# Windowed attention before two gated layers: split float32r products and DMA transposes, against native float32 products and TensorE transposes

## The chip, the cores and the metric

One Trainium2 chip, one of its cores. The metric is the device time of one execution in microseconds (us); of several executions the median is taken. TensorE (PE in the profile; PEld is its weight load), VectorE (DVE), ScalarE (ACT), GpSimd (POOL) and the DMA queue of SyncE (SP) work side by side and wait for each other by semaphores.

## What is computed

Attention over 4 batches and 8 heads, 576 positions of 64 features, with a causal window of 128 and a linear bias by distance; then two gated layers on 2304 tokens of 512 features. All in float32.

```python
scores = scale * np.matmul(q, k.transpose(0, 1, 3, 2))
mask = (rel >= 0) & (rel < window)              # window = 128
scores = np.where(mask, scores + bias[None], -1000000000.0)
attn = np.exp(scores - np.max(scores, axis=-1, keepdims=True))
attn = attn / (np.sum(attn, axis=-1, keepdims=True) + 1e-09)
x = np.matmul(attn, v)                          # to 2304 x 512
x = (x @ w_a) * (x @ w_b) @ w_out               # d_ff 1536
out = ((x @ w1) * (x @ w2) @ w3) @ w_out2       # d_ff 1024
```

## The kernel before

The attention goes by units: a unit is one batch and two neighbouring heads (`units`, 16 of them), the two heads side by side on the 128 partitions. A unit has five query blocks (`NB`), of 128 queries, the last of 64; block 0 sees one block of keys, the others two (`window`). In the last block the two heads share one tile (`nj` is 1). The blocks of a unit are taken in three runs, `RUNS = ((0, 1), (2, 3), (4,))`, so there are 48 steps, and `attention_ops` (line 652) writes the program as a pipeline over steps. In step n stand:

- what was left from the step before: the evictions of the transposed q and k (`parted`), and `pv_out` of an older run;
- `scores` and `exps` of run n, then `norms` and `probs` of run n - 1;
- the transposes of a third of the next unit's q and k (`trans` in `prep`), and loads;
- at `None`, filler: matmuls of the first weight group of the first gated layer (`Filler`, `FILL` = 2.4 us a step by its own costs), as soon as that group's weights are converted and enough tokens of x are ready; lines 546 (`g1`) and 572 (`g2_two`);
- `pv` of run n - `LAG`.

Beside the steps `side.turn()` converts weights of 64 bits to float32 (`convert`, lines 107 to 126).

Every float32 operand of a TensorE product is split into a high part in float32r and the rest. For q and k: `parted` (lines 273, 274) copies the transposed block with ScalarE to `qkh` and subtracts with VectorE to `qkl`; `scores` (line 312) adds lo·hi, hi·lo and hi·hi. The two heads stand on partitions 0 to 63 and 64 to 127 of the array. `step_exps` (lines 338, 344) adds the bias and takes the extreme value with VectorE, then the exponential with ScalarE, which also sums. `norms` (357, 360) makes the reciprocals. `probs` multiplies by them and writes the result in two float16 halves into `pp` (372, 376, 378); one DMA transpose per block (line 383, SP's queue) turns `pp` into `pt`. `pv` (line 409) takes v as three bfloat16 parts (`v_parts`, made by GpSimd at line 72) as weights and `pt` as the moving operand: five terms per key block and head, the two heads in the two halves of the array's columns. `pv_out` (423, 424) evicts to `x_hi` and `x_lo`.

Accumulation tiles in PSUM: `ps_s` has three banks (scores), `ps_t` three (tile `tr`: transposed q and k, and the output of `pv`), `ps_g` two (filler and `keep_warm`, line 353, which runs idle products in the first three units).

Behind the attention the rest of the filler runs, then the other nine weight groups in the same manner with 512 tokens per tile, and a product of the last two weights, `w34`, which is made on the way.

Of the kernel before, what the change touches and what calls it, by code (L numbers as in the profile page):

```python
# [34 lines left out]
LAG = 3  # L35
# [7 lines left out]
def attention_moe_moe(ctx, tc, q, k, v, w_a, w_b, w_o, w_1, w_2, w_3, w_o2, out):  # L43
# [10 lines left out]
    PSC = 2.0 ** 15  # L54
# [133 lines left out]
    v_raws = [raw_p.tile([P, NB, P], F32, name=f"v_raw{i}") for i in range(3)]  # L188

    def consts():  # L190
        nc.gpsimd.memset(ident, 0.0)
        nc.gpsimd.affine_select(
            out=ident, in_=ident, pattern=[[-1, P]], base=0, channel_multiplier=1,
            compare_op=ALU.not_equal, fill=1.0,
        )

        rel = raw_2.tile([P, 2 * P], F32, name="rel")
        nc.gpsimd.iota(
            rel, pattern=[[1, 2 * P]], base=-P, channel_multiplier=-1,
            allow_small_or_imprecise_dtypes=True,  # L200
        )
# [13 lines left out]

        for j in range(2):
            nc.sync.dma_start(
                out=relb2[j * LAST:(j + 1) * LAST],
                in_=relb.rearrange("p (h j) c -> p h j c", j=2)[0:LAST, :, j, :],
            )  # L220
        for t in [t for ts in raws for t in ts] + v_raws:
            nc.vector.memset(t[:, NB - 1, :], 0.0)
# [7 lines left out]
    def load_unit(u, which=(0, 1, 2)):  # L230
        b, hp = units[u]
        for x in which:
            s = (q, k, v)[x][b, 2 * hp:2 * hp + 2]
            t = raw_of(u)[x] if x < 2 else v_raws[u % 3]
            for j in range(2):
                nc.sync.dma_start(
                    out=t[:, 0:NB - 1, j * D:(j + 1) * D],
                    in_=s[j, 0:(NB - 1) * P, :].rearrange("(c p) d -> p c d", p=P),
                )
            if x:  # L240
                nc.sync.dma_start(
                    out=t[0:LAST, NB - 1, :].rearrange("p (j d) -> p j d", j=2),
                    in_=s[:, (NB - 1) * P:S, :].rearrange("j p d -> p j d"),
                )
                continue

            for j in range(2):
                o = slice(j * D, (j + 1) * D)
                nc.sync.dma_start(out=t[o, NB - 1, o], in_=s[j, (NB - 1) * P:S, :])
# [4 lines left out]
    qk, vS = {}, {}  # L254

    def prep(u):


        def part(n):
            o = slice(parts[n][0][2], parts[n][-1][2] + P)  # L260
            hold = []

            def trans():
                if n == 0:
                    qk[u] = [tr_p.tile([P, 2 * NB * P], F32R, name=f"qk{x}") for x in "hl"]
                ps = ps_t.tile([P, W], F32, name="tr")[:, 0:o.stop - o.start]
# [11 lines left out]
        def v_parts():  # L278

            vr = v_raws[u % 3]  # L280
            r1 = tr_p.tile([P, NB, P], F32, name="v1")
            v2 = tr_p.tile([P, NB, P], BF16, name="v2")
            upper = [t.bitcast(BF16).rearrange("p c (f t) -> p c f t", t=2)[:, :, :, 1] for t in (vr, r1)]
            vS[u] = upper + [v2]
            sub(nc.gpsimd, r1, vr, upper[0])
            sub(nc.gpsimd, v2, r1, upper[1])

        return [part(n) for n in range(len(parts))] + [(v_parts, None)]
# [10 lines left out]
    def scores(run):  # L299
# [4 lines left out]
        for u, i in run:  # L304
            hi, lo = qk[u]
# [13 lines left out]
    def exps(run):  # L319
        st = sm_p.tile([P, 4, 2 * len(run)], F32, name="st", bufs=4)  # L320
        at = 0
        for u, i in run:
            nj = window(i)[3]
            live[u, i]["st"] = st[:, :, at:at + nj]
            step_exps(u, i)
            at += nj
        live[run] = st[:, :, 0:at]

    def step_exps(u, i):
# [5 lines left out]
        st = d["st"]  # L335
        for j in range(nj):
# [4 lines left out]
                accum_out=st[:, 0, j:j + 1],  # L341
# [13 lines left out]
    def norms(run):  # L355
        st = live.pop(run)
        nc.vector.tensor_scalar(
            out=st[:, 2], in0=st[:, 1], scalar1=1.0e-9, scalar2=1.0 / PSC, op0=ALU.add, op1=ALU.mult
        )
        nc.vector.reciprocal(out=st[:, 3], in_=st[:, 2])  # L360

    def probs(u, i):
        m, n, nb, nj = window(i)
        d = live[u, i]
        pe, st = d["pe"], d["st"][:, 3]
        pp = sm_p.tile([P, 2 * 2 * 2 * P], F16, name="pp", bufs=5)[:, 0:2 * nj * n].rearrange(
            "p (a b c) -> p a b c", a=nj, b=2
        )

        for j in range(nj):  # L370
            if i == 0:
                nc.vector.tensor_scalar(
                    out=pp[:, j, 0, :], in0=pe[:, j, :n], scalar1=st[:, j:j + 1], scalar2=None, op0=ALU.mult
                )
            else:
                nc.scalar.activation(pp[:, j, 0, :], pe[:, j, :n], ACTF.Copy, scale=st[:, j:j + 1])
        for j in range(nj):
            nc.vector.scalar_tensor_tensor(  # L378
                out=pp[:, j, 1, :], in0=pe[:, j, :n], scalar=st[:, j:j + 1], in1=pp[:, j, 0, :],
                op0=ALU.mult, op1=ALU.subtract,  # L380
            )
        t = sm_p.tile([P, 8 * P], F16, name="pt", bufs=6)[:, 0:2 * nj * n]
        nc.sync.dma_start_transpose(
            out=t.rearrange("p (g m) -> p g m", m=P), in_=pp.rearrange("p a b c -> p (a b c)")
        )

        order = "p (a b c m) -> p a b c m" if nj == 2 else "p (b c a m) -> p a b c m"
        d["pt"] = t, t.rearrange(order, a=2, b=2, c=nb)
# [4 lines left out]
    def pv(run):  # L393


        ps = outs[run] = ps_t.tile([P, W], F32, name="tr")
        at = 0
        for u, i in run:
            vs = vS[u]
            m, n, nb, nj = window(i)  # L400
            t, pt = live.pop((u, i))["pt"]
            terms = [
                (max(i - 1, 0) + g, g, hl, z)
                for g in range(nb) for hl, z in ((0, 2), (1, 1), (1, 0), (0, 1), (0, 0))
            ]
            for x, (kb, g, hl, z) in enumerate(terms):
                for j in range(2):
                    c = slice(j * D, (j + 1) * D)
                    nc.tensor.matmul(  # L409
                        ps[c, at:at + m], vs[z][:, kb, c], pt[:, j, hl, g, :],  # L410
                        start=(x == 0), stop=(x == len(terms) - 1),
                    )
            at += m
            if u < WARM_UNITS and m == P:
                keep_warm(WARM, t[:, 0:4 * P])

    def pv_out(run):
# [4 lines left out]
        ps = outs.pop(run)[:, :m]  # L422
        nc.scalar.activation(x_hi[:, hp, o], ps, ACTF.Copy, scale=1.0 / PSC)
        nc.vector.scalar_tensor_tensor(
            out=x_lo[:, hp, o], in0=ps, scalar=1.0 / PSC, in1=f32(x_hi[:, hp, o]),
            op0=ALU.mult, op1=ALU.subtract,
        )
# [224 lines left out]
    def attention_ops():  # L652

        late = []
        for n in range(NR + LAG):
# [5 lines left out]
            if 1 <= n <= NR:  # L661
                ops.append(lambda r=runs[n - 1]: norms(r))
# [22 lines left out]
            if k == RU - 1 and u + 1 < NU:  # L685
                ops.append(trans[RU][0])
# [39 lines left out]
    for f, g in prep(0):  # L726
        f()
        if g:
            g()
# [3 lines left out]
    warm = sm_p.tile([P, 8 * P], F16, name="pt", bufs=6)[:, 0:2 * P]  # L733
    nc.vector.memset(warm, 0.0)
    keep_warm(10, warm)
# [62 lines left out]
```

## Time and profile before

| | us |
|---|---|
| median of 3 runs (993.99 to 998.30) | 995.94 |
| the profiled execution | 995.97 |
| its span, first to last instruction | 994.2 |
| PE busy in the span | 953.7 (96%) |
| DVE busy | 533.0 (54%) |
| ACT busy | 430.4 (43%) |
| POOL busy | 399.5 (40%) |

The page gives for each engine the busy time in the span; then the span in 40 slices, where each digit is a busy share in tenths (for PEclk the TensorE clock that was granted, in tenths of full speed). The end of a matmul is modelled and matmuls overlap, so that PE's rate is read from the starts of neighbouring matmuls. "SPq" is the issue of a DMA on SP's queue. The chain of waits is followed back from the last instruction, at each step to what released it.

### The profile page before, as it was taken

To read this page: it belongs to the slowest core of one execution; us is meant where nothing else is said; L and a number is where in the kernel's file an instruction comes from. 1 tells how busy PE (TensorE), PEld (TensorE's weight loads), DVE (VectorE), ACT (ScalarE), POOL (GpSimd) and SP (SyncE) were. 2 spreads that over 40 slices of the span, in tenths; PEclk is the share of its full clock that TensorE was granted. 3 is DMA by queue.
4 is the path that set the end of the run, shared out by engine and by line. 5 is a ranking of instruction groups with operands and counts; after the bars stand their busy time and mean duration, and the time that the engine had idled before them with its cause. 6 is when DMAs were issued, how large, how long until landed. Compare 5 with 4: busy or idle time off the path is not lost.

```text
span 994.2 us, 16251 instructions
## 1 busy us (share of the span) xinstructions
PE 953.7 (96%) x6162; PEld 802.6 (81%) x6162; DVE 533.0 (54%) x1188; ACT 430.4 (43%) x1003; POOL 399.5 (40%) x329
## 2 busy tenths in 40 slices
PE   8889898888999999999999999999999999999998
PEld 6558787777988788888888888888888888888886
DVE  5979877775689734566474463442442442422222
ACT  5768867775554434434443342343421321311110
POOL 4344122221688423545362362584741631611111
PEclk9968999998999999999999999999999999999999
DMA  5797786764433222323341240120120120000012
GB/s 131 163 185 154 140 140 134 141 127 85 134 121 106 85 96 84 108 75 106 97 126 59 69 139 22 43 85 1 42 85 1 51 78 1 22 1 1 26 65 101
DMA packets 160079, 85.21 MB, mean 86 GB/s; under 512 B 128001, under 2 KB 148993, under 8 KB 160001
## 3 DMA queue, kind: packets, MB, share of 16 engines
q1 hardware_dynamic: 160000, 84.18, 34.1%
q8 instruction: 48, 0.79, 0.3%
q14 instruction: 31, 0.25, 0.1%
HBM read 58.20 MB, written 8.91 MB: 68 GB/s over the span
## 4 chain that ended last, share of the span: by engine, by line
PE 79%; DMA 7%; DVE 6%; ACT 3%; issue 3%; POOL 1%; SPq 1%; POOLq 0%; ACTq 0%; DVEq 0%
PE mm L546 44%; PE mm L583 11%; PE mm L598 10%; PE mm L462 4%; DMA pt<-pp 4%; PE s L312 3%; PE tr L409 3%; PE tr L269 2%; DVE pp L378 1%; PE mm L572 1%; DVE ca L121 1%; DMA raw<-in_moe_w_a 1%; DVE ca L117 1%; POOL ca L126 1%; PE mm L454 1%
## 5 line engine op out<-in xcount | busy, mean ns | idle before, releaser
L72 POOL TENSOR_TENSOR gl<-g,gh 128x512 fp32r<-128x512 f32 (+1 forms) x108 | 123.9, 1148 | 312.4 <-ACT gh L556 312.1
L553 DVE TENSOR_TENSOR g<-a,mm 128x512 f32<-128x512 f32 (+1 forms) x108 | 64.1, 594 | 212.8 <-PE mm L546 189.8
L126 POOL TENSOR_TENSOR ca<-ca,ce 128x512 int32<-128x512 int32 x76 | 101.3, 1333 | 141.2 <-ACT ce L110 68.6
L556 ACT ACTIVATE gh<-g 128x512 fp32r<-128x512 f32 (+1 forms) x108 | 60.2, 558 | 175.6 <-DVE g L553 175.6
L546 PE MATMUL mm<-x_hi,wlA 128*128 128x512 f32 (+1 forms) x464 | 107.5, 350 | 0.0
L551 ACT ACTIVATE a<-mm 128x512 f32<-128x512 f32 (+1 forms) x108 | 56.0, 519 | 117.5 <-PE mm L546 117.4
L546 PE MATMUL mm<-x_lo,whA 128*128 128x512 f32 (+1 forms) x464 | 104.0, 345 | 0.0
L546 PE MATMUL mm<-x_hi,whA 128*128 128x512 f32 (+1 forms) x464 | 102.9, 343 | 0.0
L546 PE MATMUL mm<-x_hi,wlB 128*128 128x512 f32 (+1 forms) x400 | 99.1, 370 | 2.1 <-DVE g L553 0.8
L546 PE MATMUL mm<-x_lo,whB 128*128 128x512 f32 (+1 forms) x400 | 98.5, 368 | 0.0
L546 PE MATMUL mm<-x_hi,whB 128*128 128x512 f32 (+1 forms) x400 | 98.1, 368 | 0.0
L114 DVE TENSOR_SCALAR ca<-ca 128x512 f32<-128x512 f32 x76 | 46.3, 610 | 91.8 <-ACT ca L107 90.6
L546 PEld LDWEIGHTS mm<-x_lo,whA 128*128 128x128 f32 x464 | 78.1, 192 | 10.5
L546 PEld LDWEIGHTS mm<-x_hi,wlA 128*128 128x128 f32 x464 | 77.7, 192 | 10.8 <-issue 0.4
L546 PEld LDWEIGHTS mm<-x_hi,whA 128*128 128x128 f32 x464 | 77.3, 191 | 10.2
L546 PEld LDWEIGHTS mm<-x_hi,wlB 128*128 128x128 f32 x400 | 70.8, 188 | 15.6 <-ACT a L551 1.3
L107 ACT ACTIVATE ca<-raw 128x512 f32<-128x512 f32 x76 | 50.7, 668 | 72.1 <-DMA raw<-in_moe_w 38.2
L587 DVE TENSOR_TENSOR acc<-acc,mm 128x512 f32<-128x512 f32 (+1 forms) x100 | 61.9, 629 | 36.9 <-PE mm L583 36.6
L546 PEld LDWEIGHTS mm<-x_lo,whB 128*128 128x128 f32 x400 | 71.1, 189 | 12.6
L546 PEld LDWEIGHTS mm<-x_hi,whB 128*128 128x128 f32 x400 | 71.0, 189 | 12.5
L121 DVE SCALAR_TENSOR_TENSOR ca<-raw,ca 128x512 int32<-128x512 int32 x76 | 79.9, 1052 | 1.8
L110 ACT ACTIVATE ce<-raw 128x512 int32<-128x512 uint32 x76 | 50.9, 670 | 60.0 <-POOL ca L126 24.9
(104 smaller groups left out, 1868.7 us busy)
## 6 DMA issues: line engine op xcount, KB each, us to landing
raw<-in_moe_w SPq DMA_DIRECT2D x32, 512.0 KB, 3.7
raw<-in_moe_w_out SPq DMA_DIRECT2D x20, 512.0 KB, 3.6
raw<-in_moe_w_a SPq DMA_DIRECT2D x12, 512.0 KB, 3.6
raw<-in_moe_w_b SPq DMA_DIRECT2D x12, 512.0 KB, 3.6
out<-acc SPq DMA_DIRECT2D x18, 256.0 KB, 2.0
q_raw<-in_q SPq DMA_DIRECT2D x32, 128.0 KB, 2.9
k_raw<-in_k SPq DMA_DIRECT2D x32, 128.0 KB, 2.7
v_raw<-in_v SPq DMA_DIRECT2D x32, 128.0 KB, 2.9
```

The source lines that it names most:

```text
L72: eng.tensor_tensor(out=out, in0=a, in1=b, op=ALU.subtract)
L107: nc.scalar.activation(a, f32(hw), ACTF.Abs)
L110: nc.scalar.activation(e, lw, ACTF.Copy, scale=2.0 ** -29)
L121: nc.vector.scalar_tensor_tensor(out=ai, in0=hw, scalar=-(1 << 30), in1=ai, op0=ALU.bitwise_and, op1=ALU.bitwise_or)
L126: nc.gpsimd.tensor_tensor(out=ai, in0=ai, in1=es[0], op=ALU.add)
L546: nc.tensor.matmul(p, w[:, z, kk, :], x[:, kk, o], start=(y == 0), stop=(y == len(terms) - 1))
L551: nc.scalar.activation(a, ps[0], ACTF.Copy)
L553: nc.vector.tensor_tensor(out=gg, in0=a, in1=ps[1], op=ALU.mult)
L556: nc.scalar.activation(gh, gg, ACTF.Copy)
L583: nc.tensor.matmul(p, w, x, start=(y == 0), stop=(y == len(terms) - 1))
L587: nc.vector.tensor_tensor(out=ya, in0=ya, in1=p, op=ALU.add)
L598: nc.tensor.matmul(p, x, w, start=(y == 0), stop=(y == len(terms) - 1))
```

## The change

q and k are evicted once, in float32 (`qk`), by ScalarE or VectorE, and not split. A score is one native float32 product in place of three float32r products. The exponentials are not normalised and not split: `probs` transposes them in float32 with TensorE into a tile `tr`, from which ScalarE (blocks 1 to 3) or VectorE (blocks 0 and 4) evicts them to `pt`. `norms` is gone, and so is the sum in the exponential. v stays as loaded, in rows of 66 per head, of which the last two hold 1.0; `pv` takes `pt` as weights and v as moving operand, so that queries come out on partitions, with the sum of their exponentials in column 64. VectorE adds 1e-9, takes the reciprocal and multiplies into `y`. `pv_out` turns `y` back with TensorE, two transposes for a run of two blocks, or for the last block one native product with two stacked identities (`pair`), into the tile in which `pv`'s output stood, and evicts as before. `LAG` goes from 3 to 2. GpSimd sets the columns of ones, `y_last` and `pair` at the start.

On PE, in the middle of the attention, where a run's scores end and a `pv` begins (`s` is the score tile, `v_844`, `v_845` the lower parts of v), before:

```order
L312 MATMUL s<-qkl,qkh 128x256
L312 MATMUL s<-qkh 128x256
L312 MATMUL s<-qkh,qkl 128x256
L312 MATMUL s<-qkl,qkh 128x256
L312 MATMUL s<-qkh 128x256
L409 LDWEIGHTS v_845
L409 MATMUL tr<-pt,v_845 64x128
L409 LDWEIGHTS v_845
L409 MATMUL tr<-pt,v_845 64x128
L409 LDWEIGHTS v_844
L409 MATMUL tr<-pt,v_844 64x128
```

The change, in the same place of a later unit (`pe` are the exponentials, `y` the normalised output, `v_raw_99` v as loaded, line 538 the filler `g1`):

```order
L285 MATMUL tr<-ident,k_raw_120 128x128 x3
L378 MATMUL tr<-v_raw_99,pt 128x66 x6
L358 MATMUL tr<-ident,pe 128x128 x2
L315 MATMUL s<-qk 128x256 x5
L285 MATMUL tr<-ident,q_raw 128x128 x3
L378 MATMUL tr<-v_raw_99,pt 128x66 x6
L417 MATMUL tr<-ident,y 128x128 x2
L378 MATMUL tr<-v_raw_99,pt 128x66 x2
L358 MATMUL tr<-ident,pe 128x128 x2
L538 MATMUL mm<-x_hi,wlA_320 128x256
L538 MATMUL mm<-x_hi,wlA_567 128x256
L358 MATMUL tr<-ident,pe 128x128 x4
```

Three float32r products per score became one, ten narrow-weight pairs of `pv` per block became two or four matmuls, and transposes of `pe` and `y` stand between them.

On SP's queue, before, in the middle of the attention:

```order
L383 DMA_TRANSPOSE pt<-pp 128x4x128
L383 DMA_TRANSPOSE pt<-pp 128x8x128 x3
L236 DMA v_raw_100<-in_v 128x4x64 x2
L241 DMA v_raw_100<-in_v 64x2x64
L383 DMA_TRANSPOSE pt<-pp 128x4x128
```

The same place of the change:

```order
L246 DMA k_raw<-in_k 128x4x64 x2
L251 DMA k_raw<-in_k 64x2x64
L246 DMA v_raw_101<-in_v 128x4x64 x2
L251 DMA v_raw_101<-in_v 64x2x64
L246 DMA q_raw<-in_q 128x4x64 x2
```

The transposes of `pp` are gone from the queue, and loads alone are left.

On VectorE, between the bias instructions of two runs, before:

```order
L378 SCALAR_TENSOR_TENSOR pp<-pe,st,pp 128x128 x2
L274 TENSOR_TENSOR qkl<-tr,qkh 128x512
L378 SCALAR_TENSOR_TENSOR pp<-pe,st,pp 128x256 x2
L357 TENSOR_SCALAR st<-st 128x4
L424 SCALAR_TENSOR_TENSOR x_lo<-tr,x_hi 128x256
L360 RECIPROCAL st<-st 128x4
```

The change:

```order
L72 TENSOR_TENSOR x_lo<-tr,x_hi 128x256
L388 TENSOR_SCALAR r<-tr 128x4
L270 COPY pt<-tr 128x256
L389 RECIPROCAL r<-r 128x4
L392 TENSOR_TENSOR y<-tr,r 128x256
L72 TENSOR_TENSOR x_lo<-tr,x_hi 128x256
```

In place of the subtractions for `pp` and `qkl` stand an eviction of `pt`, the sums' reciprocal and the product `y`.

The diff, cut to its core (`load_unit` only follows the new layout of v; the score tile's `st` has one row where it had four):

```diff
--- before.py
+++ after.py
@@ constants @@
-LAG = 3
+LAG = 2
...
-    PSC = 2.0 ** 15
+    DA = D + 2
...
-    v_raws = [raw_p.tile([P, NB, P], F32, name=f"v_raw{i}") for i in range(3)]
+    v_raws = [raw_p.tile([P, NB, 2, DA], F32, name=f"v_raw{i}") for i in range(3)]
+    y_last = [raw_p.tile([P, 2, D], F32, name=f"y_last{i}") for i in range(2)]
+    pair = raw_p.tile([P, D], F32, name="pair")
+    warm = raw_p.tile([P, W], F16, name="warm")
...
+        for t in v_raws:
+            nc.gpsimd.memset(t[:, :, :, D:DA], 1.0)
+        for t in y_last:
+            nc.gpsimd.memset(t, 0.0)
+        for j in range(2):
+            o = slice(j * D, (j + 1) * D)
+            nc.gpsimd.tensor_copy(out=pair[o], in_=ident[o, o])
...
+    def evict(eng, out, in_):
+        if eng is nc.scalar:
+            eng.activation(out, in_, ACTF.Copy)
+        else:
+            eng.tensor_copy(out=out, in_=in_)
@@ prep @@
-                    qk[u] = [tr_p.tile([P, 2 * NB * P], F32R, name=f"qk{x}") for x in "hl"]
+                    qk[u] = tr_p.tile([P, 2 * NB * P], F32, name="qk")
...
             def parted():
-                hi, lo = qk[u]
-                nc.scalar.activation(hi[:, o], hold[0], ACTF.Copy)
-                nc.vector.tensor_tensor(out=lo[:, o], in0=hold[0], in1=f32(hi[:, o]), op=ALU.subtract)
+                evict(nc.scalar if n == 1 else nc.vector, qk[u][:, o], hold[0])
...
-        return [part(n) for n in range(len(parts))] + [(v_parts, None)]
+        return [part(n) for n in range(len(parts))]
@@ scores @@
-            for x, (a, b) in enumerate(((lo, hi), (hi, lo), (hi, hi))):
-                for j in range(nj):
-                    r = slice(j * D, (j + 1) * D) if nj == 2 else slice(0, P)
-                    nc.tensor.matmul(
-                        ps[j][:, at:at + n], a[r, qs], b[r, ks], start=(x == 0), stop=(x == 2)
-                    )
+            for j in range(nj):
+                r = slice(j * D, (j + 1) * D) if nj == 2 else slice(0, P)
+                nc.tensor.matmul(ps[j][:, at:at + n], t[r, qs], t[r, ks], start=True, stop=True)
@@ step_exps @@
-            nc.scalar.activation(
-                pe[:, j, :n], pe[:, j, :n], ACTF.Exp, bias=st[:, 0, j:j + 1], scale=-1.0,
-                accum_out=st[:, 1, j:j + 1],
-            )
+            nc.scalar.activation(pe[:, j, :n], pe[:, j, :n], ACTF.Exp, bias=st[:, j:j + 1], scale=-1.0)
@@ norms and the body of probs removed; probs now @@
+        pe = d.pop("pe")
+        ps = ps_t.tile([P, W], F32, name="tr")[:, 0:nj * n]
         for j in range(nj):
...
+            for g in range(nb):
+                o = (j * nb + g) * P
+                nc.tensor.transpose(ps[:, o:o + P], pe[:, j, g * P:(g + 1) * P], ident)
+        t = d["pt"] = sm_p.tile([P, W], F32, name="pt", bufs=6)[:, 0:nj * n]
+        evict(nc.vector if i in (0, NB - 1) else nc.scalar, t, ps)
@@ pv: the loop over five terms removed; now @@
+            for j in range(nj):
+                js = slice(j, j + 1) if nj == 2 else slice(0, 2)
+                for g in range(nb):
+                    q0 = (j * nb + g) * P
                     nc.tensor.matmul(
...
+                        ov[:, x, js], t[:, q0:q0 + P], v_t[:, max(i - 1, 0) + g, js],
+                        start=(g == 0), stop=(g == nb - 1),
                     )
...
+        sums = ov[:, :, :, D].rearrange("p x j -> p (x j)")
+        r = sm_p.tile([P, 2, nx], F32, name="r", bufs=4)
+        nc.vector.tensor_scalar(out=r[:, 0], in0=sums, scalar1=1.0e-9, scalar2=None, op0=ALU.add)
+        nc.vector.reciprocal(out=r[:, 1], in_=r[:, 0])
+        if window(run[0][1])[3] == 2:
+            y = sm_p.tile([P, nx, D], F32, name="y")
+            nc.vector.tensor_tensor(
+                out=y, in0=ov[:, :, :, 0:D].rearrange("p x j d -> p (x j) d"),
+                in1=r[:, 1].unsqueeze(2).to_broadcast([P, nx, D]), op=ALU.mult,
+            )
+        else:
+            y = y_last[run[0][0] % 2]
+            for j in range(2):
+                c = slice(j * D, (j + 1) * D)
+                nc.vector.tensor_scalar(
+                    out=y[c, j], in0=ov[c, 0, j, 0:D], scalar1=r[c, 1, j:j + 1], scalar2=None, op0=ALU.mult
+                )
+        outs[run] = ps, y
@@ pv_out @@
+        if m == LAST:
+            nc.tensor.matmul(ps, y, pair, start=True, stop=True)
+        else:
+            for x in range(len(run)):
+                nc.tensor.transpose(ps[:, x * P:(x + 1) * P], y[:, x * P:(x + 1) * P], ident)
+        nc.scalar.activation(x_hi[:, hp, o], ps, ACTF.Copy)
+        sub(nc.vector, x_lo[:, hp, o], ps, f32(x_hi[:, hp, o]))
@@ attention_ops @@
-                ops.append(lambda r=runs[n - 1]: norms(r))
...
-            if k == RU - 1 and u + 1 < NU:
-                ops.append(trans[RU][0])
```

## Rows read from the trace of the kernel before

**Rows 1.** The page: span, and the granted TensorE clock in 40 slices

```profile
span 994.2 us, 16251 instructions
PEclk9968999998999999999999999999999999999999
```

**Rows 2.** Busy time by stretch: PE, PEld, DVE, ACT, POOL, clock, DMA, GB/s

```profile
10.00:250.00 240.00, 208.83 (x2515) 173.33 (x2514) 185.01 (x684) 174.58 (x550) 65.33 (x57) 0.91 0.74 140
250.00:994.00 744.00, 737.89 (x3616) 623.86 (x3615) 345.10 (x494) 252.96 (x450) 325.21 (x255) 1.00 0.22 68
```

**Rows 3.** ACT in order of time, the last pv_out: start us, us

```profile
249.87 0.22 ACT L423 ACTIVATE x_hi<-tr 128x64 fp32r<-128x64 f32 x1
```

**Rows 4.** The chain of waits between 10 and 250 us, summed by line

```profile
by line: DMA pt<-pp 16.5%; PE mm L546 13.5%; PE s L312 11.6%; PE tr L409 10.7%; PE tr L269 6.9%; DVE pp L378 5.9%; PE mm L572 5.4%; issue 4.8%; DVE pe L338 2.7%; ACT pp L376 2.3%; DMA q_raw<-in_q 2.2%; SPq L236 2.0%; DMA raw<-in_moe_w_a 1.9
```

**Rows 5.** The DMA transposes of line 383: issue times, and time to landing

```profile
L383 SPq DMA_TRANSPOSE pt<-pp x80: 1188/1250/3693, 17.0 to 240.0; - x80
DMA to landing us min/median/max: 2.4/3.2/5.8
```

**Rows 6.** PE in order of time: start us, us, line, tile, shape

```profile
63.44 0.27 PE L312 MATMUL s<-qkl,qkh 64*128 64x128 f32 x2
63.55 0.28 PE L312 MATMUL s<-qkh 64*128 64x128 f32 x2
...
121.25 0.49 PE L269 MATMUL tr<-ident,k_raw 128*128 128x128 f32 x3
...
127.12 0.28 PE L312 MATMUL s<-qkh 64*128 64x256 f32 x2
127.24 0.29 PE L312 MATMUL s<-qkh,qkl 64*128 64x256 f32 x2
...
164.87 0.22 PE L409 MATMUL tr<-pt,v 128*64 128x128 f16 x2
164.93 0.22 PE L409 MATMUL tr<-pt,v_raw 128*64 128x128 f16 x2
```

**Rows 7.** The chain from 100 to 250 us, two pieces: start us, us

```profile
141.80 2.86 PE mm L546 x24
147.12 1.43 PE mm L572 x12
```

**Rows 8.** Lines 546 and 572 alone, by stretch (columns of rows 2)

```profile
0.00:100.00 100.00, 10.98 (x72) 9.64 (x72) 0.86 0.80 159
100.00:250.00 150.00, 38.17 (x266) 34.70 (x267) 0.95 0.69 126
...
0.00:100.00 100.00, 0.89 (x3) 0.48 (x3) 0.86 0.80 159
100.00:250.00 150.00, 20.99 (x141) 18.02 (x141) 0.95 0.69 126
```

**Rows 9.** Groups of one shape: busy us, mean ns | idle before

```profile
L344 ACT ACTIVATION_READ_ACCUMULATOR pe<-pe,st 128x1 f32 x144 | 27.4, 190 | 0.0
L424 DVE SCALAR_TENSOR_TENSOR x_lo<-tr,x_hi 128x256 fp32r<-128x256 f32 x32 | 13.2, 414 | 4.6 <-ACT x_hi L423 4.6
L454 PE MATMUL mm<-ident,ca 128*128 128x128 f32 x64 | 9.7, 271 | 0.0
L353 PE MATMUL mm<-pt 128*128 128x512 f16 x24 | 9.6, 491 | 0.3 <-DMA pt<-pp 0.3
L273 ACT ACTIVATE qkh<-tr 128x512 fp32r<-128x512 f32 x16 | 9.4, 589 | 6.6 <-PE tr L269 6.6
L357 DVE TENSOR_SCALAR st<-st 128x4 f32<-128x4 f32 x32 | 7.0, 218 | 6.8 <-ACT pe L344 6.7
```

**Rows 10.** Tile pp alone, 0 to 250 us: DVE busy, ACT busy

```profile
0.00:250.00 250.00, 79.66 (x176) 49.37 (x112) 0.92 0.73 139
```

**Rows 11.** Stretches of 5 us (columns of rows 2)

```profile
70.00:75.00 5.00, 5.00 (x40) 4.05 (x41) 2.32 (x13) 4.13 (x15) 1.28 (x2) 0.50 1.19 190
75.00:80.00 5.00, 5.00 (x65) 4.38 (x61) 4.27 (x20) 4.47 (x13) 0.00 (x0) 0.50 0.68 150
```

More of the change, by code (lines that the diff above doesn't have):

```diff
@@ L233, in load_unit @@
             s = (q, k, v)[x][b, 2 * hp:2 * hp + 2]
-            t = raw_of(u)[x] if x < 2 else v_raws[u % 3]
+            t = raw_of(u)[x].rearrange("p c (j d) -> p c j d", j=2) if x < 2 else v_raws[u % 3]
             for j in range(2):
                 nc.sync.dma_start(
-                    out=t[:, 0:NB - 1, j * D:(j + 1) * D],
+                    out=t[:, 0:NB - 1, j, 0:D],
                     in_=s[j, 0:(NB - 1) * P, :].rearrange("(c p) d -> p c d", p=P),
@@ L241, in load_unit @@
                 nc.sync.dma_start(
-                    out=t[0:LAST, NB - 1, :].rearrange("p (j d) -> p j d", j=2),
+                    out=t[0:LAST, NB - 1, :, 0:D],
                     in_=s[:, (NB - 1) * P:S, :].rearrange("j p d -> p j d"),
@@ L248, in load_unit @@
                 o = slice(j * D, (j + 1) * D)
-                nc.sync.dma_start(out=t[o, NB - 1, o], in_=s[j, (NB - 1) * P:S, :])
+                nc.sync.dma_start(out=t[o, NB - 1, j], in_=s[j, (NB - 1) * P:S, :])
     cols = [(x, i, (x * NB + i) * P) for x in range(2) for i in range(NB)]
     parts = [cols[0:3], cols[3:7], cols[7:10]]
-    qk, vS = {}, {}
+    qk = {}
+    def evict(eng, out, in_):
[3 more added lines that the diff above has]
+            eng.tensor_copy(out=out, in_=in_)
     def prep(u):
@@ L304, in scores @@
         for u, i in run:
-            hi, lo = qk[u]
+            t = qk[u]
             m, n, nb, nj = window(i)
@@ L323, in exps, with step_exps @@
             nj = window(i)[3]
-            live[u, i]["st"] = st[:, :, at:at + nj]
-            step_exps(u, i)
+            step_exps(u, i, st[:, at:at + nj])
             at += nj
-        live[run] = st[:, :, 0:at]
-    def step_exps(u, i):
+    def step_exps(u, i, st):
         hp = units[u][1]
@@ L353, in keep_warm @@
             nc.tensor.matmul(ps[:, :x.shape[1]], x[:, 0:P], x, start=(y == 0), stop=(y == cnt - 1))
[L355 to L360, printed above, removed]
     def probs(u, i):
@@ L364, in probs @@
         d = live[u, i]
[L365 to L368, printed above, removed]
+        pe = d.pop("pe")
+        ps = ps_t.tile([P, W], F32, name="tr")[:, 0:nj * n]
         for j in range(nj):
[L371 to L388, printed above, removed]
+            for g in range(nb):
[3 more added lines that the diff above has]
+        evict(nc.vector if i in (0, NB - 1) else nc.scalar, t, ps)
     ready = [0]
@@ L393, in pv @@
     def pv(run):
[L396 to L399, printed above, removed]
+        ps = ps_t.tile([P, W], F32, name="tr")
+        ov = ps[:, 0:len(run) * 2 * DA].rearrange("p (x j d) -> p x j d", x=len(run), j=2)
+        for x, (u, i) in enumerate(run):
             m, n, nb, nj = window(i)
[L401 to L408, printed above, removed]
+            t = live.pop((u, i))["pt"]
+            v_t = v_raws[u % 3]
+            for j in range(nj):
+                js = slice(j, j + 1) if nj == 2 else slice(0, 2)
+                for g in range(nb):
+                    q0 = (j * nb + g) * P
@@ L409, in pv @@
                     nc.tensor.matmul(
-                        ps[c, at:at + m], vs[z][:, kb, c], pt[:, j, hl, g, :],
-                        start=(x == 0), stop=(x == len(terms) - 1),
+                        ov[:, x, js], t[:, q0:q0 + P], v_t[:, max(i - 1, 0) + g, js],
+                        start=(g == 0), stop=(g == nb - 1),
                     )
-            at += m
             if u < WARM_UNITS and m == P:
-                keep_warm(WARM, t[:, 0:4 * P])
+                keep_warm(WARM, warm)
@@ L421, in pv_out @@
         o = slice(b * S + i * P, b * S + i * P + m)
[L422 to L427, printed above, removed]
+        ps, y = outs.pop(run)
+        ps = ps[:, :m]
+        y = y.rearrange("p x d -> p (x d)")
+        if m == LAST:
[5 more added lines that the diff above has]
+        sub(nc.vector, x_lo[:, hp, o], ps, f32(x_hi[:, hp, o]))
         if hp == NP - 1:
@@ L727, in attention_moe_moe @@
         f()
-        if g:
-            g()
+        g()
     load_unit(1, (0, 1))
```

19 lines of the change are left out of this document (5 added, 14 removed).

## Prediction

> **What bounds the kernel now.** I read the page first. The span is 994.2 us and the granted clock is full from slice 11 on [rows 1]; the profiled execution took 995.97 us, that is 1.8 us around its span, and the median of the three runs is 995.94, so profile and median agree. Next the busy time by stretch [rows 2]: from 250 us to the end PE is busy 737.9 of 744.0 us at clock 1.00, so that part is TensorE alone, and the change touches nothing in it. The attention ends at 249.9 us, with the last eviction of `pv_out` [rows 3]. What follows starts when attention ends (its weights and pools come then), so I take a shift of that point one for one.
>
> So the question is the 240 us from 10 to 250, in which 16 units (batch, pair of heads) pass, 15.0 us each. There no engine is full: PE's modelled busy time is 208.8, VectorE's 185.0, ScalarE's 174.6 us [rows 2], and matmuls overlap in the first of these. The chain of waits of that stretch [rows 4] tells what stands between: the DMA transposes `pt<-pp` hold 16.5% (39.6 us), the two writers of `pp` 5.9% and 2.3% (19.7 us). The queue view shows why: 80 transposes, each 1.25 us of issue and 3.2 us to landing [rows 5], and a unit has five.
>
> How much PE needs is read from starts, not from busy time [rows 6]. A pair of score products on 64 rows each starts 0.11 us after the pair before it at 128 columns (63.44, 63.55) and 0.12 at 256 (127.12, 127.24). A pair of `pv` products starts every 0.06 us (164.87, 164.93). Three float32 transposes end 0.49 us after the first began; one alone lasts 0.27 (line 454) [rows 9], so each further one costs 0.11. A filler matmul costs 2.86/24 = 0.12 [rows 7].
>
> One unit before: 10 transposes of q and k 1.1; scores 3 × 0.11 + 12 × 0.12 = 1.8; `pv` 45 pairs × 0.06 = 2.7 (the ten narrow pairs counted alike). Together 5.6 us, 90 us in 16 units. Filler in the attention: 338 matmuls of line 546 and 144 of line 572 [rows 8] × 0.12 = 58. Warming matmuls 10 (line 353) [rows 9]. That is 158 of 240 us; for 82 us PE waits, or loses by half clock.
>
> **The change, part by part.** Bounds first for what the trace doesn't show: a native float32 product. The program as built has two weight loads and two matmuls for each (its list of matmuls is longer by 416 than the kernel's, and there are 144 + 256 + 16 native products).
>
> *Scores.* A float32r product moves 256 columns in 0.12 us, and the old code needed three of them for the product of two halves by two halves with the last one dropped. A native one keeps all four: 0.48 us. Below, if it were one pass per matmul: 0.24. Above, if the two heads no longer ran side by side: 0.96 a pair. I take 0.48 a pair, and 0.3 us a unit more because the two matmuls of one head now stand next to each other, so that only neighbours of different heads overlap: two at 0.11 for block 0, then 4 × 0.48, plus 0.3 = 2.4 us (before 1.8; bounds 1.2 and 3.8, the last block having no pair).
>
> *`pv`.* 16 products of 66 or 132 columns with 128 × 128 weights. Each of the two matmuls I price as a float32 transpose, 0.11, its nearest row by weights and type: 32 × 0.11 = 3.5 us (before 2.7). Below, if loading half the bits takes half as long as in a transpose: 1.8. Above, four passes with a load each: 7.0.
>
> *Transposes of the exponentials.* 16 × 0.11 = 1.8 us. *`pv_out`.* Four transposes and one native product: 0.7. Both new. q and k as before, 1.1.
>
> Sum after: 2.4 + 3.5 + 1.8 + 0.7 + 1.1 = 9.5 us a unit, against 5.6: 3.9 × 16 = **62 us more TensorE work**, all in the stage. Bounds: the low prices give 6.6 a unit (16 us more in all), the high ones 14.4 (141 more).
>
> *DMA.* The 80 transposes go, and with them their place in SP's queue ahead of the loads of q, k, v and weights. On the chain that is the 39.6 us. Late next is the new eviction of the transposed exponentials: a ScalarE copy of 128 × 512, 0.59 us (line 273) [rows 9], a fifth of the 3.2 us.
>
> *VectorE and ScalarE.* All work on `pp` goes, 79.7 and 49.4 us [rows 10], 19.7 of it on the chain; so do the reads of the exponentials' accumulator (27.4 us of ScalarE) and the norms. Added on VectorE: 32 copies of 256 columns and 32 products `y` at some 0.41 (line 424) [rows 9], 48 times an add and a reciprocal at 0.2 each, 32 small products: about 52 us, and the subtractions of `qkl` become copies. Added on ScalarE: 48 copies of 0.59, 28 us. Both get lighter, so beside 9.5 us of PE work they hide, apart from hand-overs. GpSimd loses the split of v, which hid already. The longer v rows and the constants set at the start lie beside the first loads: nothing, while these take their 2 to 3 us.
>
> *LAG 3 to 2, and filler.* Same number of steps and same filler per step; the last `pv` comes one step sooner. I leave it in the stalls.
>
> **The sum.** PE's need after: 158 + 62 = 220 us. Of the 82 us of stalls 39.6 + 19.7 = 59 go, and 23 are left (loads, clock, hand-overs). Between none and all of it stays; with PE the fullest engine part of it falls behind PE's own work, and I take half: 12. The stage takes 232 us instead of 240: 995.97 − 8 = **988 us**. With none left 976, with all 999.
>
> **Rivals.**
>
> *Cheaper native products.* `pv` at 1.8 instead of 3.5 a unit: 27 us less PE work. PE then needs 193; with all 23 us of stalls, as it is less full, 216 instead of 240. Time 972, and with half of the stalls 961. For it: one of the two matmuls of a product uses half the bits. Against: transposes of the same type cost 0.11.
>
> *Slower, through the `tr` banks.* There are three, and a step now asks for four tiles instead of two: two of transposed exponentials, one of q and k, and one of `pv`, held until `pv_out` has written into it and been read. Held times from rows: `pv` 8 × 0.22, add and reciprocal 0.4, `y` 0.4, transposes 0.2, two evictions 0.8, about 3.6 us; the exponentials 2 × (0.44 + 0.59); q and k 0.44 + 0.59. Together 6.7 us on three banks, 2.2 a step, under PE's 3.2. It decides once hand-overs and queueing on VectorE and ScalarE add about 3 us a step, some 0.3 at each of ten. At 0.6 each it is 12.7/3 = 4.2 us a step, 1.0 more in the steps that have no filler to put there. These are half of the 48 (58 us of filler at `FILL` = 2.4 a step is 24 steps): 24 us. Time about 1010.
>
> *Slower, through the clock.* Between 70 and 80 us PE is busy all the time, when little filler ran yet (75 of its matmuls in the first 100 us [rows 8]), and the clock is 0.50, the lower of its two levels [rows 11]. If the steps without filler (24 × 3.2 = 77 us) ran so, they would take 77 us more, less the 12 of stalls: 1050; if half of them, 1015 to 1025. For it: that stretch, and that transposes grow from 10 to 30 a unit. Against: later the clock is full almost throughout [rows 1], and PE will have fewer gaps. The Trainium skill (TensorE: Matmul & The Clock Gate, Part 4: PE-mode transpose) says that transposes don't count as work for the clock in the way matmuls do; by that rule a third of the new PE work would not hold it up. No row here has transposes alone, so the trace doesn't decide it.
>
> *Dearer native products.* Scores not side by side and loads in series: some 3 us more a unit, 48 in all: about 1030.
>
> That the change doesn't do what it says I exclude: the new order holds no DMA transpose.
>
> **How the numbers follow.** Forecast 988 (976 to 999): 0.42; cheaper products 961 to 972: 0.18; banks 1000 to 1015: 0.20; clock 1015 to 1050: 0.12; dearer 1010 to 1035: 0.08. A measurement of this kernel can tell about 0.5% from no change, so 991 to 1001 is no difference. Faster: 0.25 of the forecast's cases and 0.18, 0.43. Same: 0.15 of the forecast and 0.04 of the banks, 0.19. Slower: the rest, 0.38. The range 960 to 1022 leaves out the clock at its worst, half of the dear case and a bit of the cheap one.
>
> **What would show it.** Right: the last `pv_out` near 242 us; PE starts 0.11 apart in `pv`, score pairs some 0.48; no DMA piece but loads in the chain of the stage; the part behind still 744 us. Cheap: `pv` starts near 0.06. Banks: PE waiting for evictions of `tr` in the steps without filler. Clock: more low slices in the page's row of it than the three below 9 now. Wrong altogether: a change behind 250 us.

## The result, and the profile after

The changed kernel takes **1002.11 us** (median of 6 runs, 1001.76 to 1003.14), the kernel before 995.35 on the same chip: ratio 1.0065, 95% interval 1.0048 to 1.0083. The forecast of 988 was on the wrong side; the range held the time. The profiled execution took 1001.76 us with a span of 1000.0, so 5.8 us of span are to be found.

All but 0.8 of them are in the stage of attention. The last `pv_out` in order of time, ScalarE, the kernel after (start us, us), against [rows 3]:

```profile
254.84 0.20 ACT L418 ACTIVATE x_hi<-tr 128x64 fp32r<-128x64 f32 x1
```

It comes 5.0 us later. Busy time by stretch, the kernel after (PE, PEld, DVE, ACT, POOL, clock, DMA, GB/s), against [rows 2]:

```profile
10.00:100.00 90.00, 79.92 (x596) 68.00 (x597) 53.38 (x225) 54.36 (x124) 17.78 (x16) 0.94 0.45 111
100.00:255.00 155.00, 151.58 (x1210) 134.88 (x1210) 86.13 (x367) 79.46 (x191) 7.42 (x10) 1.00 0.22 52
255.00:999.80 744.80, 736.55 (x3602) 622.20 (x3601) 347.84 (x491) 252.11 (x447) 325.04 (x256) 1.00 0.20 66
```

The last stretch is the one the prediction left alone: from the last `pv_out` to the end it takes 745.2 us, before 744.3. In the middle one TensorE is busy 151.58 of 155 us at full clock, while VectorE and ScalarE are busy only about half of the time. The kernel before, over nearly the same units:

```profile
10.00:100.00 90.00, 79.39 (x783) 59.81 (x782) 78.44 (x274) 68.73 (x212) 34.21 (x28) 0.85 0.83 163
100.00:250.00 150.00, 129.44 (x1735) 113.52 (x1734) 106.58 (x411) 105.85 (x339) 31.12 (x30) 0.95 0.69 126
```

The chain of waits from 10 to 255 us, the kernel after, against [rows 4]:

```profile
by line: PE tr L378 18.6%; PE mm L538 14.5%; PE s L315 13.8%; PE tr L358 10.3%; PE mm L564 7.5%; PE tr L285 5.0%; ACT pe L342 4.3%; DMA raw<-in_moe_w_a 3.6%; DMA raw<-in_moe_w_out 2.8%; DVE pe L336 2.8%; PE tr L417 2.5%; issue 1.9%; DMA raw
```

As forecast, no DMA piece but loads is left, and the transposes and `pp` are gone. In their place stands TensorE. Its order of time shows the prices, against [rows 6] (start us, us of the whole group, count at the end):

```profile
208.19 1.90 PE L378 MATMUL tr<-v_raw,pt 128*128 128x66 f32 x16
210.35 1.13 PE L315 MATMUL s<-qk 64*128 64x256 f32 x8
```

A group lasts from its first start to its last end, and one instruction alone 0.27 (`pv`) or 0.40 (scores), as the groups of one shape say (busy us, mean ns | idle before):

```profile
L378 PE MATMUL tr<-v_raw,pt 128*128 128x66 f32 x448 | 55.6, 273 | 3.8 <-ACT pt L268 3.0 <-DVE qk L270 0.9
L358 PE MATMUL tr<-ident,pe 128*128 128x128 f32 x256 | 43.5, 285 | 3.6 <-DVE pt L270 3.0 <-ACT qk L268 0.3 <-DVE r L389 0.2
L315 PE MATMUL s<-qk 64*128 64x256 f32 x188 | 30.9, 396 | 0.0
```

So `pv` instructions start (1.90 − 0.27)/15 = 0.11 us apart, two for each product. Of the scores, eight instructions are two pairs of products. The two heads run side by side: (1.13 − 0.40)/3 = 0.24 for each further two instructions, 0.48 a pair. Both are the prices of the prediction (0.11 and 0.48). The idle time of these lines before a releaser is small, 3.8 and 3.6 us in the whole stage.

### The profile page after: what moved, and what is told of

Read it like the earlier page. It is cut to its first block, busy times and chain, and to the rows that moved or that the text cites. A ratio compares the mean times of both kernels' runs of the same rounds, so it can differ in the third digit from the quotient of the medians.

```text
span 1000.0 us, 14206 instructions
## 1 busy us (share of the span) xinstructions
PE 975.9 (98%) x5442; PEld 830.0 (83%) x5442; DVE 489.8 (49%) x1092; ACT 387.8 (39%) x763; POOL 359.2 (36%) x304
## 4 chain that ended last, share of the span: by engine, by line
PE 87%; DVE 5%; DMA 3%; ACT 3%; issue 1%; POOL 0%; ACTq 0%; SPq 0%; DVEq 0%; POOLq 0%
PE mm L538 45%; PE mm L575 12%; PE mm L590 10%; PE tr L378 5%; PE mm L454 4%; PE s L315 3%; PE tr L358 3%; PE mm L564 2%; DMA raw<-in_moe_w_a 2%; PE tr L285 1%; ACT pe L342 1%; DMA raw<-in_moe_w_out 1%; DVE ca L121 1%; DVE ca L114 1%; DVE ca L117 1%
## 5 line engine op out<-in xcount | busy, mean ns | idle before, releaser
L114 DVE TENSOR_SCALAR ca<-ca 128x512 f32<-128x512 f32 x76 | 49.9, 656 | 82.6 <-ACT ca L107 82.5
L538 PEld LDWEIGHTS mm<-x_hi,wlA 128*128 128x128 f32 x464 | 77.4, 189 | 14.3 <-ACT x_hi L418 4.4
L342 ACT ACTIVATE pe<-pe,st 128x256 f32<-128x256 f32 (+1 forms) x144 | 60.8, 476 | 40.3 <-DVE st L336 40.2
```

The lines of the kernel that those rows point to most:

```text
L114: nc.vector.tensor_scalar(out=a, in0=a, scalar1=bits(0x38000000), scalar2=None, op0=ALU.max)
L342: nc.scalar.activation(pe[:, j, :n], pe[:, j, :n], ACTF.Exp, bias=st[:, j:j + 1], scale=-1.0)
L538: nc.tensor.matmul(p, w[:, z, kk, :], x[:, kk, o], start=(y == 0), stop=(y == len(terms) - 1))
```

## Experiments

I compare kernels by the last `pv_out`, which the text calls the end of the stage, and by the time. **Gaps** are worked out from the starts of all matmuls in the trace between 10 us and the end of the stage: of each interval from one start to the next, what exceeds 0.25 us, added up. It is 40 us in the kernel before and 19 in the kernel after. What is left is TensorE's own time, with half clock and the waits shorter than 0.25 us still in it: 240 − 40 = 200, and 245 − 19 = 226. The first five of the 16 units are called early, the other eleven late.

Theory A: TensorE bounds the changed stage. Theory B: hand-overs through PSUM banks and the short lag do. Theories C, D and E came with the results.

### Is it TensorE?

**Each native score product twice**, kernel after:

```
-            for j in range(nj):
+            for j in 2 * list(range(nj)):
```

> The changed kernel with each native score product issued twice (same result). By the starts in the trace of after this is 1.94 us more of TensorE work a unit, 31 us in 16 units. Theory A (TensorE bounds the stage from about 97 us on, and the first six units are bound by something else): the ten late units pay in full, the early ones little: 19 to 31 us above the changed kernel, 1021 to 1033 us. Theory B (hand-overs through the PSUM tiles of tr and the short lag hold the stage): less than 10 us, under 1012.

Measured 1044.68 us, ratio to the kernel before (as in all that follow) 1.0501 (1.0474 to 1.0527): 42 us above the changed kernel, more than the work was priced at (31) and more than theory A allowed. The first five units pay 16.9 of it (their last eviction comes at 116.65 instead of 99.78 us), the eleven others 26, 2.4 us each. TensorE's own time grows by 41 us, from 226 to 267, and the gaps stay (19 and 21). Theory A, and in the early units too, where it expected little.

**One split score product five times**, kernel before:

```
-            for x, (a, b) in enumerate(((lo, hi), (hi, lo), (hi, hi))):
+            for x, (a, b) in enumerate(4 * ((lo, hi),) + ((lo, hi), (hi, lo), (hi, hi))):
...
-                        ps[j][:, at:at + n], a[r, qs], b[r, ks], start=(x == 0), stop=(x == 2)
+                        ps[j][:, at:at + n], a[r, qs], b[r, ks], start=(x <= 4), stop=(x < 4 or x == 6)
```

> The kernel before with the first of the three split score products issued five times instead of once (same result): 4 more passes of 0.11 to 0.12 us a pair, 2.4 us a unit, 38 us of TensorE work in all. By the prediction's own count (82 us of the 240 in which PE waits) it should nearly disappear: 0 to 8 us above the kernel before. Theory A says that this count was wrong, PE's starts leave only about 40 us of gaps: 15 to 30 us.

Measured 1025.61 us, 1.0301 (1.0279 to 1.0323): 30 us for 38 us of work, at the upper end of what theory A allowed. But the two parts of the stage differ. The eleven late units take 6 us more for 26 us of work, so 20 us were hidden: there the kernel before did have TensorE time to spare. The first five take 22 us more for 12 us of work (the fifth ends at 118.39 instead of 96.35): own time grows by 13 us there and gaps by 9.

**`pv` in one bf16 pass**, kernel after:

```
-        t = d["pt"] = sm_p.tile([P, W], F32, name="pt", bufs=6)[:, 0:nj * n]
+        t = d["pt"] = sm_p.tile([P, W], BF16, name="pt", bufs=6)[:, 0:nj * n]
...
-            v_t = v_raws[u % 3]
+            v_t = v_raws[u % 3].bitcast(BF16).rearrange("p c j (d t) -> p c j d t", t=2)[:, :, :, :, 1]
```

> The changed kernel with the products with v in one bf16 pass: the eviction of the transposed exponentials writes bf16, and of v the upper 16 bits are read; the low bits of both are left out. 16 instead of 32 instructions a unit at 0.112 us: 1.8 us a unit less, 29 us in 16 units, more if a bf16 weight load is quicker. Theory A: 18 to 35 us below the changed kernel, 967 to 984. Theory B: under 8 us below.

Measured 979.14 us, 0.9834 (0.9814 to 0.9853): 23 us below the changed kernel, as theory A said. Here the early units get *slower*: the fifth ends at 103.96 us instead of 99.78. TensorE's own time falls in them by 11 us, but gaps rise from 12 to 28. In part of that time TensorE is busy half to seven tenths of the time and runs at less than full clock:

```profile
50.00:60.00 10.00, 5.31 (x33) 3.82 (x35) 5.56 (x21) 5.63 (x13) 4.93 (x4) 0.61 0.71 178
60.00:70.00 10.00, 7.13 (x41) 5.68 (x40) 5.44 (x21) 6.19 (x13) 4.26 (x4) 0.70 0.31 105
```

(stretches of 10 us of this run, columns as above; the kernel after has 1.00 in both.)

**Native scores alone**, kernel before:

```
-                    qk[u] = [tr_p.tile([P, 2 * NB * P], F32R, name=f"qk{x}") for x in "hl"]
+                    qk[u] = tr_p.tile([P, 2 * NB * P], F32, name="qk")
...
-            for x, (a, b) in enumerate(((lo, hi), (hi, lo), (hi, hi))):
...
+                nc.tensor.matmul(ps[j][:, at:at + n], t[r, qs], t[r, ks], start=True, stop=True)
```

> The kernel before with one part of the change alone: native float32 scores and one eviction of q and k; DMA transposes, split v and LAG 3 stay. Going back to split scores cost the changed kernel 18 us. Theory A (the native scores are a gain by themselves, and the other parts of the change lose more than that): 972 to 988 us. Theory D (they gain only where TensorE is full, the kernel before waits elsewhere): 990 to 997. The prediction's price (0.6 us a unit dearer) would give 996 to 1006.

Measured 996.21 us against 997.95 for the kernel before in the same comparison, 0.9987 (0.9967 to 1.0007): nothing, as theory D said. By the time alone the prediction's price, 996 to 1006, would do as well; but the work did not get dearer. It went (TensorE's own time falls from 200 to 186 us), and gaps took its place (40 to 53).

**Split scores back**, kernel after: the same edit the other way, all else native.

> The changed kernel with the scores back in three float32r passes of split halves, and q and k evicted twice (as before the change); all else native. The prediction priced them 0.6 us a unit cheaper than the native ones: 10 us, 992. By the starts in both traces they are dearer, 2.9 to 3.3 us a unit against 2.6, which is 5 to 11 us, and the second eviction comes on top: theory A expects 1005 to 1015.

Measured 1019.9 us, 1.0221 (1.0183 to 1.0259), 16 us (by the ratios) to 18 us (by the medians) above the changed kernel, more than either guess. TensorE's own time grows by 18 us (226 to 244), and the gaps stay. The same part is worth nothing before the change and 16 to 18 us after it. That is what a change of the bound looks like.

### Banks, lag, warming

**Four banks for `tr`, two for the scores**, kernel after (`ps_s` `bufs=3` to 2, `ps_t` `bufs=3` to 4):

> The changed kernel with four PSUM banks for tr and two for the scores (before three and three). Theory A: within 4 us of the changed kernel. Theory B (the three tr banks hold the steps): 6 to 20 us below.

Measured 996.3 us, 1.0002 (0.9986 to 1.0017), 5.8 below the changed kernel, short of what theory B asked and more than A allowed. The gain is in the first units (the fifth ends at 94.67 us instead of 99.78); from there to the end of the stage it takes 155.9 us, the kernel after 155.1. So three banks do cost something, but only early.

**LAG 3**, kernel after:

> The changed kernel with LAG 3 again (pv three steps behind the scores). Theory A (TensorE bounds the stage): 999 to 1006 us. Theory B (with a lag of 2 TensorE waits for exponentials and their evictions): 985 to 997.

Measured 1008.58 us, 1.012 (1.0096 to 1.0144): 6 us slower, 2 to 3 beyond theory A's range, in the first units (the fifth ends at 104.23). Theory B is wrong here, and the shorter lag, which the prediction left out of its sum, was a gain.

**The four banks and warming in five units** (`WARM_UNITS` 5):

> The changed kernel with four PSUM banks for tr and two for the scores, and warming matmuls in five units instead of three (16 more of them, 3.5 us at full clock). If half clock in units 3 and 4 is what is left to win there: 988 to 994 us. If the warming is only more TensorE work: 997 to 1002.

Measured 997.02 us, 1.0006 (0.9992 to 1.002): no gain over the banks alone.

### What were the removed parts worth?

**pv waits for no transpose**, kernel before:

```
+    fixed = raw_p.tile([P, 8 * P], F16, name="fixed")
...
+        t = fixed[:, 0:2 * nj * n]
         d["pt"] = t, t.rearrange(order, a=2, b=2, c=nb)
```

> The kernel before with its DMA transposes issued as they were, but pv reads a constant table in place of what they write (four result tiles instead of six, for room): the transposed exponentials are left out of the result. So TensorE waits for no transpose. The prediction's count (39.6 us of the chain are the transposes' and go with them): 952 to 962 us. Theory E (TensorE's starts without gaps add up to 200 of the 240 us, not 158, so that only part of 40 us of gaps can go): 970 to 985.

Measured 990.23 us, 0.9933 (0.9907 to 0.9958): 6.7 us, less than both theories. The wait that held 16.5% of the chain is worth a sixth of its 39.6 us. The stage itself ends 14.3 us earlier (235.61 instead of 249.87), all of it in the late units; but 42 filler matmuls that ran in the stage before come behind it now, and what lies behind takes 751.8 us instead of 744.3. What is late next shows in the early stretch of this run, where VectorE is busy 82.57 of 90 us:

```profile
10.00:100.00 90.00, 68.55 (x796) 54.30 (x796) 82.57 (x272) 67.75 (x214) 34.05 (x27) 0.83 0.87 167
100.00:236.00 136.00, 124.51 (x1690) 109.22 (x1686) 105.42 (x411) 103.14 (x334) 30.46 (x29) 0.93 0.73 131
```

The fifth unit ends at 96.48 us, in the kernel before at 96.35.

**Neither transposes nor `pp`**, kernel before: the two loops that write `pp` and the DMA transpose are left out, `pv` reads `fixed`.

> As the run before, and the two writers of pp and the DMA transposes left out altogether (pv reads the constant table): what the change removes is gone, and nothing that it adds is there. The prediction's count (59 us go): 932 to 945 us. Theory E (no more than the 40 us of gaps can go, and half clock takes some back): 958 to 978.

Measured 958.95 us, 0.9617 (0.9587 to 0.9647): **38 us**. Last `pv_out` and stretches of this run:

```profile
205.72 0.21 ACT L404 ACTIVATE x_hi<-tr 128x64 fp32r<-128x64 f32 x1
```

```profile
10.00:100.00 90.00, 75.44 (x942) 62.23 (x943) 55.93 (x228) 58.12 (x192) 34.68 (x30) 0.87 0.49 119
100.00:206.00 106.00, 104.62 (x1563) 93.00 (x1562) 64.84 (x285) 72.37 (x249) 30.12 (x29) 1.00 0.29 69
```

With transposes and `pp` gone and nothing added, TensorE is full from 100 us on (104.62 of 106). Theory E: there was no more to win than until TensorE is the bound. The stage ends 44 us earlier, the time falls by 38: 19 filler matmuls come behind the stage, TensorE is idle there for 9.2 us instead of 6.3, and the part behind takes 751.0 us instead of 744.3. This run splits the change in two: without transposes and `pp` the time is 38 us lower, and all the rest of the change costs 1002 − 959 = 43.

Of the 44 us the eleven late units give 32, and TensorE does in them the same work as in the kernel before: it takes 5.9 us of its own time a unit, at clock 1.00, where the kernel before took 6.8. The first five give 12; 18 us of gaps stay in them.

**Idle DMA transposes**, kernel after, on a constant table, into tiles that nobody reads; two result tiles, then six:

```
+        idle = sm_p.tile([P, 8 * P], BF16, name="idle", bufs=2)[:, 0:w2]
+        nc.sync.dma_start_transpose(
+            out=idle.rearrange("p (g m) -> p g m", m=P),
+            in_=relb.rearrange("p h c -> p (h c)")[:, 0:w2],
+        )
```

> The changed kernel with the 80 DMA transposes issued again at their old place, each on a constant table and into a tile that nobody reads: as many and as large as before, but no one waits for them. Theory A (what the transposes cost before was hidden behind work or paid back by TensorE): 0 to 6 us above the changed kernel. Rival C (their room in SP's queue and on the DMA engines cost the kernel before 10 to 30 us by late loads, and the change did win that): 1012 to 1030.

> The changed kernel with the 80 DMA transposes that nobody reads once more, with six result tiles instead of two, so that no transpose waits in SP's queue for the one two before it. Theory C (the transposes cost the kernel by their room in SP's queue and on the DMA engines, whoever waits for them): 1015 to 1035 again. Theory A (that cost came from the two tiles, which hold up the loads behind them): 1002 to 1012.

Measured 1036.74 us (1.0407, 1.038 to 1.0434) and 1025.71 (1.0288, 1.0271 to 1.0304). Both lie far above theory A's ranges, the second inside theory C's. The trace shows where: with six tiles the fifth unit ends 4.8 us later (104.56), the next six keep pace, and then one hole costs 18 us. Pieces of the chain there (start us, us):

```profile
191.75 2.01 PE tr L384 x16
193.83 1.29 SPq L361
195.16 1.26 SPq L361
...
203.26 1.26 SPq L361
...
207.13 2.81 DMA q_raw<-in_q
209.95 0.14 issue
210.08 0.87 PE tr L285 x3
```

Eight transposes (line 361), each 1.3 us of issue, stand on SP's queue ahead of the load of q that TensorE waits for. So transposes do cost by their room in the queue, as rival C says, where a load that is needed soon stands behind them. What they cost the kernel before in this way isn't shown by these runs; in its chain the loads of q hold 2.2% and the issue at line 236 2.0%, together 10 us [rows 4].

### A kernel that beats both

**Keys on the rows**: the scores are computed transposed, so that the exponentials come out as `pv` wants them.

```
-                nc.tensor.matmul(ps[j][:, at:at + n], t[r, qs], t[r, ks], start=True, stop=True)
+                    nc.tensor.matmul(
+                        ps[j][:, o], t[r, k0:k0 + P], t[r, i * P:(i + 1) * P], start=True, stop=True
+                    )
...
+            nc.vector.tensor_tensor(out=pe[:, j, :n], in0=ps[j], in1=bias, op=ALU.add)
+        nc.scalar.activation(pe[:, 0:nj, :n], pe[:, 0:nj, :n], ACTF.Exp, scale=1.0 / float(D) ** 0.5)
```

> The changed kernel with the scores computed with keys on the rows, so that the exponentials need no transpose and no eviction; the row maximum is not subtracted (that part of the computation is left out: a row's largest score is then bounded only by the inputs). 16 transposes a unit go, 2.06 us of TensorE's starts in the late units, and 5 evictions. Theory A: 2.06 x 16 = 33 us at most, less what half clock takes back in the early units: 968 to 985 us. Theory B: no more than 10 us below the changed kernel.

Measured **980.98 us**, 0.9844 (0.9824 to 0.9865): 21 us below the changed kernel, 15 below the one before. From the fifth unit's end (94.31) to the stage's (234.71) it takes 140.4 us instead of 155.1, 1.3 us less for each of eleven units. Not all of it need be the transposes': VectorE's bias instruction no longer takes the extreme value, and one instruction makes the exponentials of both heads. The early units gain 5.5, though the lower clock stands in them (two stretches of 10 us, columns as above). Since the row's maximum isn't subtracted, the kernel holds for scores as small as these inputs give.

```profile
40.00:50.00 10.00, 9.24 (x44) 8.01 (x45) 9.38 (x25) 5.07 (x12) 3.92 (x3) 0.51 0.90 229
50.00:60.00 10.00, 9.63 (x48) 8.77 (x49) 6.70 (x16) 5.51 (x11) 3.46 (x3) 0.50 0.36 91
```

**The same with LAG 1:**

> The kernel with keys on the rows (no transposes of exponentials, row maximum left out), with LAG 1: pv one step behind the scores. If TensorE's work alone sets it, within 3 us of the same kernel with LAG 2 (978 to 984 us); if the hand-over from scores to pv needs two steps, 985 to 1000; if the start of the stage is paid by the lag, as LAG 3 against 2 in the changed kernel says (6 us), 973 to 978.

Measured 981.17 us, 0.9831 (0.9809 to 0.9852): the same.

**The same with four banks for the scores, two for `tr`:**

> The kernel with keys on the rows (row maximum left out) with four PSUM banks for the scores and two for tr, since the transposed exponentials no longer ask for any. If the banks of the scores hold the first units: 972 to 978 us; if tr's do: 984 to 992; if neither, 979 to 983.

Measured 1007.88 us, 1.0105 (1.0056 to 1.0153), 27 us slower, a miss, far above all three guesses. Gaps rise from 11 to 28 us. Two banks for `tr` seem too few even with half as many tiles asked for; which wait fills the gaps was not followed.

## Why the prediction was wrong

**What failed** is the step "Of the 82 us of stalls 39.6 + 19.7 = 59 go", with half of the other 23 put behind PE's own work. The sum for the stage was 240 − 70 (59, and half of the other 23) + 62 = 232 us. The run without transposes and `pp` gives the terms: 240 − **44** = 196 us without the removed parts, and + **49** to the 245 of the changed kernel. Both terms were too large, the gain by 26 us, the added work by 13. That the second error took back half of the first is luck. The range held the time because it was made wide for the rivals, and of these only the banks came, in part.

- *The 82.* It is 240 less 158 us, and 158 is a number of instructions times their shortest distance [rows 6]. What is over holds waits and, as the prediction says itself, half clock. Gaps alone are 40 us. By the starts of all matmuls late units take 6.8 us instead of 5.6 (scores 2.7, not 1.8; `pv` 3.1, not 2.7), and the first five 10.5, with half clock in them [rows 11]. The 5.6 itself was close: the same work takes 5.9 a late unit once nothing waits. What was wrong was to treat the 82 as one store over the whole stage, from which the two pieces take what they hold of the chain.
- *The 59.* In the late units the waits went almost wholly: of 22 us of gaps 1.5 stay, and 32 us are won. In the first five only 12 us are won, and 18 of 18 us of gaps stay. A share of the chain is time that a piece stood last, not time that its removal gives: the transposes' 39.6 us gave 7 of the time, 14 of the stage. Only with `pp` and the transposes' room in the queue gone as well did 38 come.
- *The added work.* The prices of the late units were nearly right: `pv` 3.5 us a unit as forecast, scores 2.1 (2.4), transposes of the exponentials 1.7 (1.8), `pv_out` 0.7, q and k 1.0 (1.1), together 9.0 against 9.5. Against the 5.9 of the run without `pp` that is 3.1 us more a unit, not 3.9, and 49 us in 16 units, not 62. From the run without `pp`, in which TensorE's own time is 176 us, to the kernel after, with 226, it grew by 50. From the kernel before, with 200, it grew by 26 alone: half clock and short waits between starts, which the 200 still holds, went while the new work came.
- *The stalls that stay.* "I take half: 12." They are 19, 12 of them in the first 90 us, where TensorE is busy 79.92.
- *Filler and what lies behind the stage* stayed as said: 495 filler matmuls run in the stage instead of 481, 1.7 us at 0.12, and the part behind takes 0.8 us more.

**The rivals.** Cheaper native products: no, `pv` starts 0.11 apart. Dearer: no. Clock: no; the kernel after has 0.94 up to 100 us and 1.00 behind, better than before (0.85 and 0.95). The Trainium skill (TensorE: Matmul & The Clock Gate, Part 4: PE-mode transpose), which the prediction cites, says that transposes don't count as work for the clock in the way matmuls do. The 30 transposes a unit stand beside other matmuls here, and this trace shows the clock full with them (1.00 from 100 to 255 us); transposes alone are in no run. Banks: partly. A fourth bank gives 5.8 us, a quarter of that rival's 24, and in the first five units alone.

**What stays open.** The parts of the added 43 us, undone one at a time, do not add up (transposes and evictions of the exponentials 21, half of `pv` 23, native scores −16 to −18, the LAG −6, and `pv_out` not tried), and why they don't was not tried; each may be paid at another clock and against another bound. Between the two runs on the removed parts, the writers of `pp` went from VectorE and ScalarE and the transposes from SP's queue; which of the three was late next wasn't separated (VectorE's 82.57 of 90 us speaks for it in the first units). Which wait holds the 12 us of early gaps in the changed kernel was not tried by itself beyond the banks. In the chain from 10 to 100 us loads of the first weight group hold 7.7, 5.7 and 4.4%, together 16 us, and no run took these away.

## What to carry to other kernels

A share of the chain of waits is not what removing that piece gives: here 59 us of the chain gave 38. To price it, look for what is nearly as late and take the smaller distance, and do it for each part of the stage by itself: where the waits went wholly (the late units) TensorE's own work was left, and where something else held the stage (the first units) most of them stayed. Time of an engine above its instructions' shortest distance is not all slack: part of it is a lower clock, and part are waits on other things. Where a change moves work onto the engine that then becomes full, price the two halves by themselves, and look for a form of the product that needs no transpose before making the transpose faster.

## What the runs showed of the hardware

- A native float32 product of two heads on 64 rows each runs side by side as split ones do, and at 256 columns costs 0.48 us a pair. In the changed kernel that is less than the three float32r passes (2.1 us a late unit against 2.6 in the run with split scores back, both at clock 1.00). In the run without transposes and `pp`, also at clock 1.00, the split passes took 2.1 us too, so what is cheaper depends on the matmuls around them.
- Less work on TensorE need not end sooner: with `pv` in one pass its own time in the first five units fell by 11 us, yet they took 4 us longer, as gaps rose by 15 us; the clock fell to 0.61 and 0.70 between 50 and 70 us. What the clock alone cost there wasn't separated.
- DMA transposes that nobody waits for still cost: 1.3 us of SP's queue each. Where eight of them stood ahead of a load of q, that unit took 18 us longer.
